# Retention attention with a bilinear feed-forward layer: slots 8 to 11 as one tile, two pairs of blocks by seven products in both four-slot tiles, and the order of all work written anew

## The chip, the cores and the metric

The kernel runs on one core of a Trainium2 chip. The metric is the device time of one execution in microseconds; the time of a kernel is the median of its runs. TensorE is called PE (its weight loads PEld), VectorE DVE, ScalarE ACT, GpSimd POOL, and SyncE, which issues the DMAs, SP.

## The reference

For each of 4 batches and 8 heads the attention runs a recurrence over 768 tokens with a head width of 64; its output is the input of the feed-forward layer.

```python
state = gamma[h] * state + k_t (outer) v_t          # 64 x 64, gamma[h] = 1 - 2**(-5-h)
y_t = (q_t @ state) / sqrt(64)                      # for each batch, head and token
x = y.transpose(0, 2, 1, 3).reshape(3072, 512)      # tokens x (heads * 64)
out = ((x @ w_a) * (x @ w_b)) @ w_out               # 512 -> 1536 -> 512, f32
```

## The kernel before

**Slots and tiles.** The 3072 tokens are 24 slots of 128, six to a batch. The feed-forward layer works on tiles of slots, TILES (line 16): 4, 2, 2, 2, 2, 4 and 8 slots, which are called tiles 0 to 6 here: tile 0 has slots 0 to 3, tile 1 slots 4 and 5, tile 2 slots 6 and 7, tile 3 slots 8 and 9, tile 4 slots 10 and 11, tile 5 slots 12 to 15, tile 6 slots 16 to 23.

**Attention of a slot.** k and q arrive by DMA as f32 and are multiplied by a table of powers of gamma into one bf16 tile `kqb` (`scaled`, lines 317 and 335); v is cast to bf16 (`vb`, line 287). SP's DMA transpose of `kqb` gives `kqT` (`flip`, line 376). On PE follow, for each slot:

- *scores*: 32 matmuls `at` (line 415) from `kqT`; DVE multiplies them by a mask into `aT` (line 421).
- *update*: 8 matmuls `st` (line 433) that add k times v to the state; a cast copies the state to `gst`.
- *inter*: 8 matmuls `y` from the state before (line 453); *intra*: 8 matmuls `y` from `aT` (line 463).
- *leave*: ACT copies `y` of a pair of slots into `xt`, the transposed input of the feed-forward layer.

`turn(new, old)` (line 477) writes these for a pair of new slots and a pair of old ones as one unbroken stretch of PE, a *burst*: update of `new`, scores of `new+1` and `new`, inter of both old slots, update of `new+1`, intra of both old slots, leave. The outputs of a pair are in the burst after the one that has its scores.

**Feed-forward.** d_ff is 12 blocks of 128. Of a block, `ffn_a` makes a with four matmuls over the tile's columns (line 619, 128 columns to a slot), which ACT copies to `asb` (line 622); `ffn_g` makes g (line 631), and DVE multiplies it by `asb` into `ht` (line 633). The banks of both come from a ring of three (line 78). The output is `ht` times w_out. For all tiles but the first this is done by seven products in place of eight (`Group`, line 717): `hs` are sums of quarters of `ht` (`hsum`, on POOL or DVE by an argument), `wsum` sums of quarters of w_out (`weight_sum`, on DVE), the products `mA`, `mB`, `mC` are matmuls of 256 columns (line 739), copied by ACT to `snaps` and added by DVE into `osb`, which `store` sends out.

**Seven products for x w_a and x w_b.** The same is done for two blocks at once (p and p+6) with halves of the tile. It needs sums of quarters of the weights (`weight_piece`, line 861, on POOL) and of the tile (`x_sum`, `xf_sum`, on DVE). Tile 6 does all six pairs of blocks so (`Unit`, `u`, line 913, 512 columns). Tile 5 does two of six pairs (`Quad`, line 1003, 256 columns), a and b apart; the remaining eight blocks are plain.

**Order.** The order on each engine is the order in which the program calls these functions, lines 1138 to 1297; `seq` ties each instruction to the one before it on its engine. The body is hand-written: `blocks(J, a, b)` writes a-blocks and g-blocks in turn, `casts(t)` the scaling of slot t, its transpose and the loads of slot t+2, `turn` a burst; `laced` writes tile 4's output between tile 5's Quads from the string LACED, and `big` the last part from the strings START and END. All scalings of slots 8 to 23 and most casts are on POOL.

```python
    turn(14, 12)
    hsum(4, 3, 0, 6, G_)
    weight_pieces(4)
    blocks(4, 6, 8)
    v_cast(16)
    blocks(4, 8, 9)
    hsums(4, 0, 3, G_)
    casts(18)
    blocks(4, 9, 10)
```

Of the kernel before, what the change touches and what calls it, by code (L numbers as in the profile page):

```python
# [9 lines left out]
F32 = mybir.dt.float32  # L10
# [5 lines left out]
TILES = [4, 2, 2, 2, 2, 4, 8]  # L16
# [3 lines left out]
START = ("A1 A2 u0.1 u1.1 A6 T X3 A7 B1 X2 A5 B6 B7 X1 A3 B5 u0.2 u1.2 B2 X4 A4 u0.6 B3 u1.6 B4 u0.5 u1.5 "  # L20
         "u0.7 u2.1 u0.3 u1.7 u2.6 u1.3 u0.4 u2.2 u3.1 u2.5 u1.4 u2.7 u3.6")
END = ("u11.1 u10.5 u10.7 u9.4 u11.6 u10.3 u11.2 S03 a1< u11.5 u11.7 u10.4 b1< u11.3 a1> b1> c1< d1< u11.4 a7 c1> d1> c2 d2 "
       "S02 S01 b7 a2 b2 S04 a6 b6 S13 a5 b5 S12 a3 b3 a4 b4 S11 c7 d7 c6 d6 S14 c5 d5 "
       "c3 c4 d4 d3")
V_LATE = range(12, 20)
LACED = ("X3 X2 m1 m7 m2 a1 b1 a2 b2 m6 X1 a6 b6 a7 b7 F2 X4 m5 a5 b5 K20 G2 a3 b3 a4 b4 V18 "
         "m3 c1 d1 F3 H3 c2 d2 c6 d6 c7 d7 c5 d5 m4 c3 d3 V19 c4 d4 G3")
# [4 lines left out]
def kernel(  # L32
# [78 lines left out]

    def raw_tile(shape, dtype, tag, name):
        return raw.tile(shape, dtype, tag=tag, name=name, bufs=3 if tag == "vf" else 2)
# [3 lines left out]
    def load_slot(t, names="kqv"):  # L117
        b, ci = divmod(t, NCH)
        for nm in names:
            src = {"k": k, "q": q, "v": v}[nm]  # L120
            if nm == "q":
                if t % 2 == 0:
                    load_two(nm, src, b, ci // 2, t)
                continue
            if t % 2 == 0:
                whole[nm] = raw_tile([P, 2, H, D], F32, nm + "f", nm + "f")
            raws[nm, t] = whole[nm][:, t % 2]
            s = src[b, :, ci * P : (ci + 1) * P, :].rearrange("h p d -> p h d")
            seq(nc.sync.dma_start(out=raws[nm, t], in_=s))

    def load_slots(t):
        for u, names in ((t, "kq"), (t + 1, "k"), (t, "v"), (t + 1, "v")):
            load_slot(u, names)
# [43 lines left out]
    def issue_loads(n):  # L177
        for _ in range(min(n, len(pending))):
            what = pending.pop(0)
            n = int(what[1:])  # L180
            if what[0] in "ab":
                load_wide(what[0], n)
            elif what[0] in "kqv":
                load_pair_q(n) if what[0] == "q" else load_two(what[0], {"k": k, "v": v}[what[0]], 0, n, 2 * n)
            else:
                {"p": load_pair, "s": load_slots, "t": load_slot, "w": load_w, "o": load_o}[what[0]](n)


    kqb = {}
# [113 lines left out]
    def cast_o(j):  # L303
        cast(nc.gpsimd, wo_bf[:, j * FPO : (j + 1) * FPO, :], wst["o", j])
# [12 lines left out]
    def scaled(eng, t, i):  # L317
        if i and t < 2 * PAIRS:
# [12 lines left out]
        else:  # L331
            dst = dst.rearrange("p hp r d -> p r hp d")
# [3 lines left out]

    def new_nat(t):
        kqb[t] = nat.tile([P, 2, HP, 2, D], BF16, tag="kqb", name="kqb")
        kb[t], qb[t] = kqb[t][:, 0], kqb[t][:, 1]
        vb[t] = nat.tile([P, H, D], BF16, tag="vb", name="vb")  # L340

    def casts(t, between=lambda: None):
        new_nat(t)
        scaled(nc.gpsimd, t, 0)
        between()
        scaled(nc.gpsimd, t, 1)
        if t not in range(12, 20):
            cast(nc.gpsimd, vb[t], raws["v", t])
        u = t + 2
        if u == 20:  # L350
            load_slot(u, "kq")
        flip(t)
        if u == 20:
            load_slot(u + 1, "k")
            return
        if u == 21:
            load_slot(u - 1, "v")
            load_slot(u, "v")
            load_slot(22, "kq")
            return  # L360
        if u in V_LATE:
            if u == 13:
                load_slot(12, "q")
            elif u == 19:
                load_slot(18, "kq")
            load_slot(u, {12: "k", 18: ""}.get(u, "kq"))
            if u % 2:
                load_slot(u - 1, "v")
                load_slot(u, "v")
        elif u < NSLOT:  # L370
            load_slot(u)

    def flip(t):
        if t % 2 == 0:
# [4 lines left out]

    def late_kq(t):  # L380
        for u in (t, t + 1):
            new_nat(u)
            scaled(nc.gpsimd, u, 0)
            scaled(nc.gpsimd, u, 1)
            flip(u)
        if t == 20:
            load_slot(23, "k")
            load_slot(22, "v")
            load_slot(23, "v")

    def casts_two(t):
        for u in (t, t + 1):
            new_nat(u)
            scaled(nc.gpsimd, u, 0)
            scaled(nc.gpsimd, u, 1)
            flip(u)
        for u in (t, t + 1):
            cast(nc.gpsimd, vb[u], raws["v", u])
        load_slot(t + 3)
# [9 lines left out]
    def scores(t, where, cuts=2):  # L409
        at = score_banks(where)  # L410
# [13 lines left out]
    def update(t, eng):  # L424
        ci = t % NCH
        if ci == NCH - 1:
            return
# [17 lines left out]

    def inter(t):
        if t % NCH == 0:
            return
        for j in range(2):
# [8 lines left out]
    def intra(t):  # L458
        for r in range(2):
# [7 lines left out]
    def leave(t):  # L467
        J, i = where[t]
# [7 lines left out]

    def turn(new, old, eng=nc.scalar):
        if old is not None:
# [844 lines left out]
```

## Time and profile before

| | before |
|---|---|
| time, median of 3 runs | 218.27 us (217.76 to 218.32) |
| the profiled execution's own time | 218.26 us |
| its span | 216.6 us |
| busy: PE, PEld | 209.8 us (97%), 145.8 us |
| busy: DVE, ACT, POOL | 151.1 us (70%), 105.1 us (49%), 155.5 us (72%) |
| granted TensorE clock | 1.00 |
| read from HBM, written | 28.31 MB, 6.29 MB |

The span runs from the first to the last instruction that the profile shows; the device time holds 1.66 us more. PE counts as busy from a matmul's start to its modelled end, and matmuls overlap, so a matmul's own length is longer than the distance from its start to the next one's start. The chain of waits follows the work that ended last backwards, at each step to what released it; its rows here are given in order of time with their length.

### The profile page before, as it was taken

What the parts mean: (1) busy time and instruction counts of PE and PEld (TensorE: products, weight loads), DVE (VectorE), ACT (ScalarE), POOL (GpSimd) and SP (SyncE); (2) the same over time, 40 slices, a digit from 0 to 9 for tenths busy, and PEclk for the clock granted to TensorE, in tenths of its full rate; (3) what the DMA queues carried; (4) which work ended last, traced back from release to release, by engine and by line L of the source; (5) the groups of instructions that cost most, each with busy time, mean ns of one, the idle gap of its engine ahead of it and who ended that gap; (6) DMA issues with size and microseconds to landing.
All of it is one profiled execution on the core that took longest, in us unless ns stands there. A gap on an engine that the chain in (4) does not pass through costs nothing.

```text
span 216.6 us, 5726 instructions
## 1 busy us (share of the span) xinstructions
PE 209.8 (97%) x2250; PEld 145.8 (67%) x2250; DVE 151.1 (70%) x277; ACT 105.1 (49%) x236; POOL 155.5 (72%) x187
## 2 busy tenths in 40 slices
PE   7789999999999999999999999999999999999994
PEld 3458445587458888888888877557864444458883
DVE  5796347845985486356377978686577887688952
ACT  3175325343224444464576475657545656652331
POOL 7277877778889487979959979799996999530000
PEclk9999999999999999999999999999999999999999
DMA  6999999999999999399989999980013000000055
GB/s 181 315 337 370 377 360 357 363 237 240 227 267 235 173 254 280 76 189 257 213 187 227 222 200 215 236 139 3 5 73 122 0 0 3 2 0 0 27 194 170
DMA packets 82906, 39.68 MB, mean 183 GB/s; under 512 B 57536, under 2 KB 75840, under 8 KB 82880
## 3 DMA queue, kind: packets, MB, share of 16 engines
q1 hardware_dynamic: 82736, 39.26, 74.4%
q8 instruction: 17, 0.28, 0.5%
q10 hardware_dynamic: 144, 0.07, 0.1%
q14 instruction: 9, 0.07, 0.1%
HBM read 28.31 MB, written 6.29 MB: 160 GB/s over the span
## 4 chain that ended last, share of the span: by engine, by line
PE 91%; SPq 3%; DMA 3%; POOL 0%; issue 0%; DVE 0%
PE a L619 18%; PE g L631 18%; PE mA L739 12%; PE uA L913 10%; PE mB L739 6%; PE o L656 5%; PE uB L913 5%; DMA wsta<-in_moe_w_a_dram 3%; PE mC L739 3%; PE at L415 2%; PE uC L913 2%; SPq L150 2%; PE y L463 2%; PE st L433 2%; PE fa L1003 2%; SPq L138 1%
## 5 line engine op out<-in xcount | busy, mean ns | idle before, releaser
L633 DVE TENSOR_TENSOR ht<-g,asb 128x256 bf16<-128x256 f32 (+1 forms) x70 | 34.4, 493 | 30.3 <-PE g L631 27.1
L619 PE MATMUL a<-xt,wa_bf 128*128 128x256 bf16 (+1 forms) x280 | 48.6, 300 | 0.2 <-POOL wa_bf L287 0.2
L631 PE MATMUL g<-xt,wb_bf 128*128 128x256 bf16 (+1 forms) x280 | 48.4, 300 | 0.0
L622 ACT CAST asb<-a 128x256 bf16<-128x256 f32 (+1 forms) x70 | 30.0, 428 | 33.5 <-PE a L619 31.3
L631 PEld LDWEIGHTS <-wb_bf 128*128 128x128 bf16 x280 | 27.1, 98 | 10.2
L619 PEld LDWEIGHTS <-wa_bf 128*128 128x128 bf16 x280 | 26.5, 98 | 10.8 <-POOL wa_bf L287 0.6
L920 ACT COPY snap<-uA 128x512 f32<-128x512 f32 x36 | 20.0, 587 | 15.4 <-PE uA L913 13.9
L335 POOL TENSOR_TENSOR kqb<-kf,ktab 128x512 bf16<-128x512 f32 x22 | 22.9, 1045 | 5.3 <-DMA kf<-in_k_dram 4.9
L739 PEld LDWEIGHTS <-hs 128*128 128x128 bf16 x234 | 22.8, 98 | 3.6
L421 DVE TENSOR_TENSOR aT<-at,mask 128x512 bf16<-128x512 f32 x36 | 22.3, 683 | 0.3
L335 POOL TENSOR_TENSOR kqb<-qf,qtab 128x512 bf16<-128x512 f32 x18 | 19.8, 1100 | 2.6 <-DMA qf<-in_q_dram 1.6
L672 POOL TENSOR_TENSOR ht<-gsb,asb 128x512 bf16<-128x512 bf16 x13 | 15.2, 1174 | 7.5 <-DVE gsb L672 7.4
L746 ACT COPY snaps<-mA 128x256 f32<-128x256 f32 x30 | 11.0, 374 | 18.9 <-PE mA L739 18.9
L672 POOL TENSOR_TENSOR hs<-ht 128x384 bf16<-128x384 bf16 (+3 forms) x14 | 15.8, 1130 | 5.7 <-DMA kf<-in_k_dram 3.2
L739 PEld LDWEIGHTS <-ht 128*128 128x128 bf16 x180 | 17.5, 98 | 3.3
L672 POOL TENSOR_TENSOR hs<-ht,hs 128x384 bf16<-128x384 bf16 (+1 forms) x17 | 16.8, 993 | 2.5 <-DVE ht L633 2.3
L739 PE MATMUL mA<-wsum,hs 128*128 128x256 bf16 x120 | 15.2, 273 | 0.0
L672 DVE TENSOR_TENSOR osb<-mB,snaps 128x256 f32<-128x256 f32 x20 | 8.4, 422 | 8.2 <-ACT snaps L746 4.3
L287 POOL CAST vb<-vf 128x512 bf16<-128x512 f32 x12 | 7.8, 668 | 5.2 <-DMA vf<-in_v_dram 5.2
L656 PE MATMUL o<-wo_bf,ht 128*128 128x512 bf16 x48 | 10.7, 379 | 0.0
L672 DVE TENSOR_TENSOR gsb<-uB,snap 128x512 bf16<-128x512 f32 x12 | 8.2, 686 | 2.9 <-ACT snap L920 2.1
L672 DVE TENSOR_TENSOR asb<-uB,snap 128x512 bf16<-128x512 f32 x12 | 8.2, 685 | 2.9 <-ACT snap L920 2.0
(148 smaller groups left out, 379.8 us busy)
## 6 DMA issues: line engine op xcount, KB each, us to landing
out_dram<-osb SPq DMA_DIRECT2D x21, 256.0 KB, 3.9
kf<-in_k_dram SPq DMA_DIRECT2D x18, 256.0 KB, 4.9
qf<-in_q_dram SPq DMA_DIRECT2D x9, 512.0 KB, 5.8
vf<-in_v_dram SPq DMA_DIRECT2D x18, 256.0 KB, 5.1
wsta<-in_moe_w_a_dram SPq DMA_DIRECT2D x6, 512.0 KB, 7.2
wsto<-in_moe_w_out_dram SPq DMA_DIRECT2D x6, 512.0 KB, 8.7
wstb<-in_moe_w_b_dram SPq DMA_DIRECT2D x5, 512.0 KB, 7.9
kf<-in_k_dram SPq DMA_DIRECT2D x3, 512.0 KB, 7.4
```

Of the source, the lines that this page charges most:

```text
L335: seq(eng.tensor_tensor(dst, src, tab, op=ALU.mult))
L421: seq(nc.vector.tensor_tensor(aT[t][:, r], at[r], mask.to_broadcast([P, HP, P]), op=ALU.mult))
L619: seq(nc.tensor.matmul(a, wa_bf[:, kt, fs], xcols(J, kt, c0, c1), start=(kt == 0), stop=(kt == KT - 1)))
L622: seq(nc.scalar.copy(asb, a))
L631: seq(nc.tensor.matmul(g, wb_bf[:, kt, fs], xcols(J, kt, c0, c1), start=(kt == 0), stop=(kt == KT - 1)))
L633: seq(nc.vector.tensor_tensor(ht[J][:, ft, c0:c1], g, asbs.pop((J, ft, c0)), op=ALU.mult))
L656: seq(nc.tensor.matmul(o, ht[J][:, ft, i * P : (i + 1) * P], wo_bf[:, ft], start=(ft == 0), stop=(ft == NFT - 1), skip_group_check=True))
L672: seq(eng.tensor_tensor(dst, x, y, op=op))
L739: seq(nc.tensor.matmul(m, w, right[:, j], start=(first and j == 0), stop=(j == NP - 1), skip_group_check=True))
L746: seq(nc.scalar.copy(self.snaps[:, n], self.bank["A"]))
L913: seq(nc.tensor.matmul(m, w, right[:, k], start=(first and k == 0), stop=(k == 1), skip_group_check=True))
L920: seq(nc.scalar.copy(self.snaps[n], self.bank["A"]))
```

## The change

**Tiles.** TILES is 4, 2, 2, 4, 4, 8: slots 8 to 11 are one tile (the new tile 3), whose blocks have 512 columns; slots 12 to 15 are tile 4 and slots 16 to 23 tile 5.

**Two of six pairs by products.** `Quad` is replaced by `Duo`, which is used in tiles 3 and 4 (pairs 0 and 1 of each). It has the a and the b product of a pair in one bank, 256 columns each, so that ACT copies, and DVE adds, 512 columns at once; a product of a and b is then one multiplication of the halves of `ab`, on DVE or POOL.

**Order.** One string, ORDER, gives all steps behind the start of tile 1, each step by a letter and numbers, and a loop calls a function for each. What `turn` wrote together are steps of their own: U update, S scores, I inter, N intra, L leave. So are k, y and v (scaling of k, of q, cast of v, with the engine: D for DVE, G for POOL, A for ACT), f (transpose), l (load), s (store), a and g (blocks), M (Group), d (Duo), u (Unit), h, x, X, W and w (the sums). `need` and `done` only assert at build time that a step stands behind those that it reads.

**Engines.** Eleven weight pieces and more `hs` sums than before are on DVE; one sum of w_out (W.1) is on POOL; four scalings (k of slot 6, q of slots 7, 10 and 17) are on ACT, where `scaled` writes eight multiplications of 128x64, and three (k of 17 and 22, q of 21) on DVE. The part before tile 1 is the same.

```diff
-TILES = [4, 2, 2, 2, 2, 4, 8]
+TILES = [4, 2, 2, 4, 4, 8]
...
+ORDER = """
...
+h.3.3.4.6.D s k.17.D l.k.19 s y.18.G g.3.11 g.3.10 h.3.4.0.4.D k.18.G f.17 M.3.0.7 l.q.20 h.3.2.4.6.G
+M.3.0.1 h.3.1.4.6.D h.3.4.4.6.D I.15 v.16.G I.14 N.14 f.18 l.v.19 l.q.22 U.15.A N.15 L.14 l.k.20 M.3.0.2
+l.v.20 M.3.0.6 y.19.G x.4.3.G k.19.G l.k.21 S.17.y.2 l.v.21 f.19 S.16.at.2 U.16.A M.3.0.5 l.k.22 x.4.2.D
...
     def scaled(eng, t, i):
...
+            if eng is nc.scalar:
+                for h in range(H):
+                    seq(nc.scalar.mul(dst[:, h % HP, h // HP, :], src[:, h, :], tab[:, h, :]))
+                return
...
-    def casts(t, between=lambda: None):
...
-    def turn(new, old, eng=nc.scalar):
...
-    def laced(order):
...
-    class Quad:
...
+    class Duo:
...
+        def product(self, bank, left, right, first):
+            if first:
+                pool, tag = self.tags[bank]
+                self.bank[bank] = pool.tile([P, 4 * P], F32, tag=tag, name="f" + bank)
+            p = self.p
+            for n, w_ in enumerate("ab"):
+                m = self.bank[bank][:, n * DH : (n + 1) * DH]
...
+                for k in range(2):
...
+                    seq(nc.tensor.matmul(m, w, right[:, k], start=(first and n == 0 and k == 0), stop=(k == 1),
+                                         skip_group_check=True))
...
+        def leave(self, i, c, bank, n):
+            ab = asbp.tile([P, 4 * P], BF16, tag="asb", name="ab")
+            tt(ab, self.bank[bank], self.snaps[n], ALU.add)
+            ft = NP * i + self.p
...
+            tt(ht[self.J][:, ft, c * DH : (c + 1) * DH], ab[:, :DH], ab[:, DH:], ALU.mult, self.engines["CBA".index(bank)
+               if bank == "C" else 1 + int(n == 1)])
...
-    def big():
...
-    turn(14, 12)
-    hsum(4, 3, 0, 6, G_)
-    weight_pieces(4)
-    blocks(4, 6, 8)
...
+    STEPS = {
+        "a": lambda J, ft: ffn_a(int(J), int(ft)),
...
+        "U": lambda t, e: update(int(t), engine[e]),
+        "S": lambda t, where, cuts: scores(int(t), where, int(cuts)),
+        "I": lambda t: inter(int(t)),
+        "N": lambda t: intra(int(t)),
+        "L": lambda t: leave(int(t)),
+    }
+    for step in ORDER.split():
+        kind, *args = step.split(".")
+        STEPS[kind](*args)
```

**Where instructions stand.** The rows give line, operation, output and inputs, and the shape; left-out rows are "...".

*PE, where the scores of slots 14 and 15 are.* Before, in `turn(14, 12)` behind a 256-column block of tile 4 (`g` with `wb_bf`): the update of 14 (`st`) opens the burst, the scores of 15 (`at_2174`) follow, and those of 14 and the outputs of 12 and 13 come behind them.

```order
L631 LDWEIGHTS wb_bf
L631 MATMUL g<-xt,wb_bf 128x256
L433 LDWEIGHTS kqb
L433 MATMUL st<-vb,kqb 64x64
...
L415 LDWEIGHTS kqT
L415 MATMUL at_2174<-kqT 64x128
L415 LDWEIGHTS kqT
L415 MATMUL at_2175<-kqT 64x128
```

Now, behind a 512-column block of tile 3: the scores of 15 (`at_2102`) and the update of 14 stand alone between two blocks; the scores of 14 and what was left of the outputs of 12 and 13 are in a burst three blocks ahead (S.14 I.13 N.12 N.13 U.13 in ORDER).

```order
L657 LDWEIGHTS wb_bf
L657 MATMUL g<-xt,wb_bf 128x512
L445 LDWEIGHTS kqT
L445 MATMUL at_2102<-kqT 64x128
...
L467 LDWEIGHTS kqb
L467 MATMUL st<-vb,kqb 64x64
...
L644 LDWEIGHTS wa_bf
L644 MATMUL a<-xt,wa_bf 128x512
```

One turn has become two bursts. Counted over the program behind 42 us, the bursts are 11 before and 16 now, and the places where one kind of matmul follows another in or beside a burst are 39 before and 47 now.

*SP, round the transpose of slot 17* (the second `DMA_TRANSPOSE` before, the first now). Before:

```order
L129 DMA kf<-in_k_dram 128x8x64
L138 DMA qf<-in_q_dram 128x8x128
L376 DMA_TRANSPOSE kqT<-kqb 128x8x128
L129 DMA kf<-in_k_dram 128x8x64
L376 DMA_TRANSPOSE kqT<-kqb 128x8x128
L129 DMA vf<-in_v_dram 128x8x64 x2
```

Now:

```order
L188 DMA vf<-in_v_dram 128x8x64
L188 DMA kf<-in_k_dram 128x8x64
L425 DMA_TRANSPOSE kqT<-kqb 128x8x128
L198 DMA qf<-in_q_dram 128x8x128
L425 DMA_TRANSPOSE kqT<-kqb 128x8x128
```

The load behind the transpose of slot 17 is now a q load of two slots, in place of v loads of one slot each.

*DVE, where k of slot 17 is scaled now* (`kqb` from `kf`). It was on POOL, between products of `ht` and the scalings of other slots.

```order
L659 TENSOR_TENSOR ht<-g,asb 128x512
L451 TENSOR_TENSOR aT<-at_2102,mask 128x512
L451 TENSOR_TENSOR aT<-at_2103,mask 128x512
L659 TENSOR_TENSOR ht<-g,asb 128x512
L696 TENSOR_TENSOR hs_1991<-ht 128x512
L403 TENSOR_TENSOR kqb<-kf,ktab_376 128x2x4x64
L659 TENSOR_TENSOR ht<-g,asb 128x512 x2
```

It stands behind the masks of slot 15, the product of block 5 and an `hs` sum.

606 lines of the change are left out of this document (249 added, 357 removed).

## The prediction

> **What bounds the kernel now.** I read the page first: the busy shares, the slices, and the split of the chain of work that ended last.
>
> ```profile
> span 216.6 us, 5726 instructions
> PE 209.8 (97%) x2250; PEld 145.8 (67%) x2250; DVE 151.1 (70%) x277; ACT 105.1 (49%) x236; POOL 155.5 (72%) x187
> PE   7789999999999999999999999999999999999994
> PE 91%; SPq 3%; DMA 3%; POOL 0%; issue 0%; DVE 0%
> ```
>
> PE is busy from the fourth slice to the last and makes 91% of the chain. PE never lets another engine onto the path, so the time is the sum of its stream: what each matmul takes, what a change between kinds of matmul costs, and the few short waits. The table by stage asks the same of the other engines (pairs: busy us, instructions; PE, PEld, DVE, ACT, POOL).
>
> ```profile
> 42.00:60.00 18.00, 18.00 (x132) 12.79 (x132) 12.51 (x21) 5.63 (x14) 14.36 (x16) 1.00 1.10 240
> 60.00:96.00 36.00, 35.99 (x448) 29.91 (x447) 22.18 (x45) 16.37 (x41) 27.85 (x33) 1.00 1.09 213
> 118.00:148.00 30.00, 30.00 (x386) 20.10 (x386) 24.50 (x46) 18.32 (x43) 27.29 (x30) 1.00 0.98 196
> 195.00:216.60 21.60, 18.42 (x171) 15.99 (x168) 14.82 (x27) 5.66 (x16) 0.00 (x0) 1.00 0.28 98
> ```
>
> PE fills every stage at a granted clock of 1.00. POOL is the next fullest (27.29 of 30.00), then DVE (24.50 of 30.00); ACT has room. A move from POOL to DVE or ACT therefore gains nothing by itself; it can only prevent or cause waits of PE. I work against the profiled execution, 218.26 us with 216.6 of span; the median of the runs is 218.27, so no correction is needed. All PE rows up to a(1,0), at about 42 us, and the last 85 are the same in both kernels, and so is what follows the last matmul; the change acts between.
>
> **Full-size matmuls.** The chain in order of time has long runs, from which one matmul is read: 7.77/36 = 0.2158 us at 512 columns, 3.93/36 = 0.1092 at 256.
>
> ```profile
> 52.75 7.77 PE o L656 x36
> 201.60 3.93 PE mA L739 x36
> ```
>
> Slots 8 to 11 as two tiles took 2 x 12 blocks x (a, g) x 4 = 192 matmuls of 256 columns. As one tile they take 8 plain blocks x 2 x 4 = 64 of 512, and two pairs of blocks by products: 2 x 2 weights x 7 x 2 = 56 of 256. The other four-slot tile had its two pairs already. So -192 x 0.1092 + 64 x 0.2158 + 56 x 0.1092 = -20.97 + 13.81 + 6.12 = **-1.04 us**.
>
> **Switches of shape.** The attention matmuls use part of the array: st and the last y are 128*64, at and the first y 64*64, all else 128*128. From the timeline of PE (start, its own length, line):
>
> ```profile
> 35.37 1.03 PE L619 MATMUL a<-xt,wa_bf 128*128 128x512 bf16 x4
> 36.33 0.64 PE L538 MATMUL at<-kqT 64*64 64x128 bf16 x32
> 36.90 0.82 PE L631 MATMUL g<-xt,wb_bf 128*128 128x512 bf16 x3
> ...
> 131.97 1.03 PE L631 MATMUL g<-xt,wb_bf 128*128 128x512 bf16 x4
> 132.93 0.32 PE L433 MATMUL st<-vb,kqb 128*64 128x64 bf16 x8
> 133.18 0.64 PE L415 MATMUL at<-kqT 64*64 64x128 bf16 x32
> 133.65 0.39 PE L453 MATMUL y<-kqT,gst 64*64 64x128 bf16 x16
> 133.97 0.32 PE L433 MATMUL st<-vb,kqb 128*64 128x64 bf16 x8
> 134.12 0.62 PE L463 MATMUL y<-aT,vb 128*64 128x128 bf16 x16
> 134.67 1.04 PE L619 MATMUL a<-xt,wa_bf 128*128 128x512 bf16 x4
> 135.54 1.03 PE L631 MATMUL g<-xt,wb_bf 128*128 128x512 bf16 x4
> ```
>
> Read from start to start. Four full matmuls take 0.87 (134.67 to 135.54), but 0.96 when a burst of attention follows (131.97 to 132.93; 35.37 to 36.33 too). Eight st take 0.15 when the shape stays (133.97) and 0.25 when it changes behind them (132.93). Thirty-two at take 0.47 with their own shape behind them (133.18) and 0.57 with a full matmul behind them (36.33). So a switch costs about 0.10 where it is plainly seen; the entry into 64*64 adds a few hundredths within the at. I take 0.12.
>
> The order counts them behind the first 42 us: before, 11 bursts with 39 switches; now, 16 bursts with 47, since a pair's update, scores and outputs no longer stand in one turn. The 8 more are 4 into 64*64 from full, 3 back, and 1 into st. 8 x 0.12 = **+0.96 us**. The bounds are nothing (if a switch costs only where something else is short) and 8 x 0.15 = 1.2. The matmuls in the bursts are the same in kind and number.
>
> The Trainium skill, TensorEngine Tiling (Array Packing), Key Properties, says that a change of the tiling mode, and not only of the tile, drains the TensorE; it gives no price. By that rule each added switch pays, and the sum has the +0.96; without it, nothing. The 0.10 at each kind of boundary above agrees with the rule.
>
> **Waits that go.** PE's own short waits show in the chain as runs longer than their like: 0.44 is four matmuls of 256, 0.57 a run of at between full matmuls.
>
> ```profile
> 43.03 0.55 PE a L619 x4
> 43.58 0.44 PE g L631 x4
> ...
> 80.62 0.66 PE at L415 x32
> 99.65 0.51 PE g L631 x4
> 113.02 0.51 PE g L631 x4
> 113.53 0.55 PE a L619 x4
> 116.27 0.66 PE at L415 x32
> ```
>
> 0.11 + 0.09 + 0.07 + 0.07 + 0.11 + 0.09 = 0.54 us. All lie in tiles of 256 columns, where a block must get its bank back in a few 0.44s. Three lie in tiles 3 and 4 of before, whose blocks become 512 wide. There the bank's work per block grows less than PE's:
>
> ```profile
> L633 DVE TENSOR_TENSOR ht<-g,asb 128x512 bf16<-128x512 f32 x18 | 12.3, 690 | 10.0 <-PE g L631 9.8
> L622 ACT CAST asb<-a 128x512 bf16<-128x512 f32 x18 | 10.6, 586 | 13.4 <-PE a L619 12.6 <-issue 0.6
> ```
>
> 0.690 and 0.586 stand against 4 x 0.2158 = 0.86. The others stand next to an attention burst whose neighbours are now different. I credit **-0.45**; the ends are -0.54 and 0, if as many come back elsewhere.
>
> **A wait that comes: the transpose of slot 17.** Before, k and q of slot 17 were scaled on POOL; now k is on DVE behind ht of block 5 and an hs sum, and the transpose follows in SP's queue. PE's steps between the end of g.3.5 and the scores of 17 are a.3.11, g.3.11, g.3.10 (12 x 0.2158 = 2.59), four products M.3.0 (24 x 0.1092 = 2.62), and a burst of 16 y from gst, 16 y and 8 st (0.32 + 0.55 + 0.15, and 0.10 to enter): 6.33 us. Against it:
>
> ```profile
> L672 DVE TENSOR_TENSOR hs<-ht 128x512 bf16<-128x512 bf16 x1 | 1.0, 1043 | 0.0
> L335 DVE TENSOR_TENSOR kqb<-kf,ktab 128x512 bf16<-128x512 f32 x2 | 1.3, 688 | 0.6 <-DMA kf<-in_k_dram 0.6
> DMA to landing us min/median/max: 3.0/4.5/6.0
> ```
>
> 0.69 + 1.04 + 0.69 = 2.42 and a landing of 3.0, 4.5 or 6.0 make 5.4, 6.9 or 8.4: a wait of 0, 0.6 or 2.1. DVE's operations overlap by some hundredths, so I take **+0.3**. Behind PE's wait stands all that follows, and nothing gives it back.
>
> **Edits that I cost at nothing.** Five weight pieces move from POOL to DVE between 42 and 60 us; at the 1.04 of the hs row they add 5.2 to DVE's 12.51 of 18, while one of four output-weight sums leaves it. That cover is gone if such a piece takes over 1.1 us more. Four scalings go to ACT in eight pieces of 64 columns. No row shows those; the nearest is this one at 128:
>
> ```profile
> L805 ACT COPY osb<-mA 128x128 f32<-128x128 f32 x1 | 0.3, 265 | 1.3 <-PE mA L800 1.3
> ```
>
> Between 8 x 0 and 8 x 0.265 = 2.1 us each I take 1.7; ACT was busy 16.37 of 36 between 60 and 96. Where a cast of a-block follows such a set, PE can lose some tenths; what hides it is the three banks of the ring. The loads issued earlier have buffers to fill only when the scalings have read them, as before. At the end the hs sums of slots 20 to 23 stand in another order on DVE, each done before its product in the same positions; no time.
>
> Sum: 218.26 - 1.04 + 0.96 - 0.45 + 0.3 = **218.0 us**.
>
> **Rivals.** *Switches nearly free.* If an added switch costs little, because the lone bursts fall where a drain hides, and slot 17 lands in 3 to 4 us, the sum is 218.26 - 1.04 - 0.45 = 216.8, and half the price gives 217.2. For: the added ones are of kinds of which before has few. Against: the 0.10 stands above at both entries into a burst and behind the st and the at of it.
>
> *Slot 17 late (slower).* The landing of 6.0, the largest of 18, makes the wait 2.1 instead of 0.3: 219.8. It decides for slower from a landing of about 5.2. For: a load of 512 KB of q is issued right behind it. Against: no load is issued in the microseconds ahead.
>
> *DVE behind.* In the pair of slots 16 and 17 four masks, two xf sums and the Duo's additions come close together. Two bf16 sums show what POOL at work does to DVE:
>
> ```profile
> L672 DVE TENSOR_TENSOR hs<-ht 128x768 bf16<-128x768 bf16 x2 | 2.3, 1132 | 0.0
> L672 DVE TENSOR_TENSOR hs<-ht 128x1536 bf16<-128x1536 bf16 x4 | 3.8, 952 | 0.1
> ```
>
> Half the columns took longer beside a working POOL than twice as many at the end, where POOL did nothing. If three such sums each come 0.5 late ahead of a product, 219.5. The Trainium skill, GPSIMD Engine Reference, Specifications, states that GpSimd's SBUF interface is shared with VectorE, with contention when a DVE instruction has two SBUF inputs; every moved sum has two. These rows agree.
>
> *It does not do what it says:* the waits of 0.54 return in the same number, 218.5.
>
> **How the numbers follow.** The forecast, 217.6 to 218.6 with its own bounds, has 0.48; switches nearly free 0.27; slot 17 late 0.13; DVE behind 0.08; the waits return 0.04. A measurement of this kernel tells about 0.3%, 0.65 us, from no change. Faster than that takes the first rival and a little of the forecast: 0.30. Slower takes the two late ones and a part of the forecast's upper end: 0.23. Between them 0.47. The range cuts off the far half of the first rival and the far end of the late ones: 217.1 to 219.3.
>
> **What would show it.** Right: PE still over 95% busy; start to start 0.96 ahead of each lone burst; the span at 216.3; no run of 0.51 or 0.55 in the new tile 3. The first rival: four full matmuls ahead of a burst at 0.87. The second: a gap of PE over 0.5 at the scores of slot 17, ended by DMA kqT. The third: gaps ended by DVE xf or ab. The forecast is wrong if PE stands still anywhere for over 0.7 us, or if a lone burst costs under half of what the rows say.

## The result, and the profile after

The changed kernel takes 218.91 us (median of 22 runs, 218.23 to 220.22) where the kernel before takes 218.07 (22 runs): ratio 1.0043, 95% interval 1.0029 to 1.0057. It is slower by 0.8 to 0.9 us. The time lies in the stated range, 217.1 to 219.3; but the sum of the prediction, 218.0, is level with before, and the kernel is slower by more than the interval. Its profiled execution was one of its longer ones, 219.68 us, so a second profile of the same kernel (218.59 us) is used beside it. The ratios leave out runs that count as disturbed, and the medians given with the experiments include them.

The page of the changed kernel: span, busy shares, and the split of the chain that ended last.

```profile
span 217.9 us, 5509 instructions
PE 208.7 (96%) x2162; PEld 138.1 (63%) x2178; DVE 162.1 (74%) x286; ACT 108.5 (50%) x246; POOL 139.1 (64%) x160
PE 72%; DMA 10%; POOL 6%; SPq 4%; issue 4%; DVE 1%; ACT 1%; POOLq 0%; DVEq 0%; ACTq 0%
```

PE is as busy as before, 96% for 97%, and this number hides the whole loss. The chain shows that there is one: PE was 91% of it and is 72%; DMA and POOL have 16%. It does not show its size: the second profile, 1.1 us shorter, has PE at 83%. By stage (columns as before: pairs of busy us and instructions for PE, PEld, DVE, ACT, POOL):

```profile
42.00:60.00 18.00, 17.87 (x161) 12.54 (x163) 12.54 (x22) 9.46 (x30) 14.33 (x13) 1.00 0.99 220
60.00:96.00 36.00, 35.54 (x436) 27.78 (x427) 27.11 (x47) 18.66 (x47) 27.44 (x27) 1.00 1.06 234
96.00:118.00 22.00, 21.41 (x290) 12.86 (x293) 18.89 (x33) 11.32 (x27) 14.98 (x15) 1.00 1.11 210
118.00:148.00 30.00, 29.22 (x324) 19.69 (x324) 23.95 (x42) 16.78 (x35) 17.72 (x21) 1.00 0.89 181
```

PE stands still for 0.46 us in the second row, 0.59 in the third and 0.78 in the fourth, where before it was busy for 35.99, 22.00 and 30.00. (The counts of matmuls are not to be compared, for some records are missing: the fourth row has 324 of PE, and e8 below, with the same order, 391.) POOL has far less work in the fourth (17.72 for 27.29), and yet POOL waits longer than before, as its waits from 42 to 148 us show, first before, then after (engine, line, what it waited for: total us, times, longest):

```profile
POOL kqb L335 <- DMA kf<-in_k_dram: 3.6, 4, 1.5
POOL kqb L335 <- DMA qf<-in_q_dram: 1.6, 3, 0.7
```

```profile
POOL kqb L403 <- DMA kf<-in_k_dram: 7.6, 4, 4.9
POOL kqb L403 <- DMA qf<-in_q_dram: 6.3, 3, 3.6
```

The scalings of k and q waited for their loads 5.2 us in all before, none over 1.5, and 13.9 now, up to 4.9. These rows are only those in which the profile names a load ahead of a scaling; before, it also names a load of k ahead of one `hs` sum and one product of `ht`, which read no k (3.2 and 1.4 us). POOL and DVE run in order, so what stands behind such a scaling is late with it. PE's three longest waits for another engine between 42 and 200 us, first profile:

```profile
PE g L657 <- DVE ht L696: 0.5, 1, 0.5
PE mA L758 <- POOL hs L696: 0.4, 1, 0.4
PE fB L1007 <- DVE xf L696: 0.2, 1, 0.2
```

Behind each of them a scaling stood for its load. Each row of the timelines below has its start, its length, and in brackets the idle time ahead of it and who ended it. **The hs sum** (the second of the three waits), in the second profile, POOL and then PE:

```profile
111.90 1.04 POOL L403 TENSOR_TENSOR kqb<-qf,qtab 128x512 bf16<-128x512 f32 x1 [3.52 <-DMA qf<-in_q_dram]
112.90 1.49 POOL L403 TENSOR_TENSOR kqb<-kf,ktab 128x512 bf16<-128x512 f32 x1
114.35 1.33 POOL L696 TENSOR_TENSOR hs<-ht,hs 128x512 bf16<-128x512 bf16 x1
```

```profile
114.43 0.60 PE L758 MATMUL mA<-wsum,hs 128*128 128x256 bf16 x4
115.74 0.39 PE L758 MATMUL mA<-wsum,hs 128*128 128x256 bf16 x2 [0.71 <-POOL hs L696]
```

y.18 waits 3.52 us for the load of q 18; k.18 and the sum h.3.2.4.6 stand behind it, and the fifth matmul of M.3.0.6 needs that sum. From start to start PE lost 0.87 us here (1.31 for 4 x 0.109), and 0.55 in the first profile. There the profile puts the same wait of y.18, 3.19 us, down to a matmul of PE; but the load of q 18 was issued at 105.69 and took 6.4 us to land, and y.18 began at 112.23, 0.14 behind the landing, as in the second profile.

Next on PE stand the scores of 17, and in the second profile their transpose was as late as the sum (PEld is PE's weight load):

```profile
116.16 0.48 PEld L445 LDWEIGHTS <-kqT 64*64 64x64 bf16 x32 [0.31 <-DMA kqT<-kqb]
```

The transpose was issued at 110.82 and landed 5.3 us later, at 116.12. PE lost another 0.10 for it (0.42 from the fifth matmul to the scores, 0.32 in the first profile), and it would have lost the whole 0.98 at the scores if the sum had been in time, for they could not begin before 116.16. So in this profile one of the two waits hides the other. In the first profile the transpose took 4.1 us and landed at 115.57, 0.27 ahead of where PE would have been without the wait for the sum. **k 22** on DVE, first profile:

```profile
132.17 1.23 DVE L403 TENSOR_TENSOR kqb<-kf,ktab 128x512 bf16<-128x512 f32 x1 [1.95 <-DMA kf<-in_k_dram]
...
133.66 0.41 DVE L696 TENSOR_TENSOR ht<-fA,asb 128x256 bf16<-128x256 f32 x1
134.12 0.81 PE L657 MATMUL g<-xt,wb_bf 128*128 128x512 bf16 x3 [0.51 <-DVE ht L696]
```

DVE stood 1.95 us for the load of k 22, a slot whose scores PE reaches at 148, and the product that gives PE its bank back (133.66) came after it. From start to start PE lost 0.68. **The xf sum**, first profile:

```profile
81.98 1.04 POOL L403 TENSOR_TENSOR kqb<-qf,qtab 128x512 bf16<-128x512 f32 x1 [2.07 <-DMA qf<-in_q_dram]
...
83.93 1.05 DVE L696 TENSOR_TENSOR hs<-ht,hs 128x384 bf16<-128x384 bf16 x1 [1.29 <-POOL hs L696]
...
86.19 1.02 DVE L696 TENSOR_TENSOR xf<-xf,xt 128x512 bf16<-128x512 bf16 x1
86.21 0.38 PE L1007 MATMUL fB<-xf,wea 128*128 128x256 bf16 x2 [0.25 <-DVE xf L696]
```

Two hand-overs: y.12 waits for q 12, the sum h.2.2 stands behind it on POOL, h.2.4 on DVE waits for h.2.2, and the xf sums stand behind h.2.4. PE lost 0.41.

The whole difference can be laid out in a sum. From the starts of all matmuls behind 42 us I took, for each kind, the number times the steady distance (0.2158, 0.1092, and 0.014 to 0.028 for those of attention), at each change of shape the usual extra of its kind (0.09 to 0.12), and called the rest waiting. The waits are thus what is left over; that the steady distances hold is seen apart from the sum, 0.216 and 0.109 in the median of all four profiles:

| us | before | after | after, second | e8 below |
|---|---|---|---|---|
| own time | 218.26 | 219.68 | 218.59 | 217.95 |
| tile 1 starts at | 41.99 | 41.76 | 41.49 | 42.00 |
| matmuls at steady distance | 165.97 | 164.93 | 164.93 | 164.93 |
| changes of shape | 39: 4.13 | 47: 4.90 | 47: 4.90 | 47: 4.90 |
| waits | 0.82 | 2.70 | 1.92 | 0.71 |

### The profile page after: what moved, and what is told of

Read it like the earlier page. It is cut to its first block, busy times and chain, and to the rows that moved or that the text cites. A ratio compares the mean times of both kernels' runs of the same rounds, so it can differ in the third digit from the quotient of the medians.

```text
span 217.9 us, 5509 instructions
## 1 busy us (share of the span) xinstructions
PE 208.7 (96%) x2162; PEld 138.1 (63%) x2178; DVE 162.1 (74%) x286; ACT 108.5 (50%) x246; POOL 139.1 (64%) x160
## 4 chain that ended last, share of the span: by engine, by line
PE 72%; DMA 10%; POOL 6%; SPq 4%; issue 4%; DVE 1%; ACT 1%; POOLq 0%; DVEq 0%; ACTq 0%
PE g L657 14%; PE a L644 13%; PE uA L908 9%; PE mA L758 9%; PE o L680 5%; PE uB L908 5%; DMA kf<-in_k_dram 4%; PE mB L758 4%; DMA wsta<-in_moe_w_a_dram 3%; POOL kqb L403 3%; DMA qf<-in_q_dram 3%; PE uC L908 2%; PE mC L758 2%; SPq L210 2%; POOL hs L696 2%
## 5 line engine op out<-in xcount | busy, mean ns | idle before, releaser
L659 DVE TENSOR_TENSOR ht<-g,asb 128x256 bf16<-128x256 f32 (+1 forms) x54 | 29.3, 550 | 17.5 <-PE g L657 16.1
L657 PE MATMUL g<-xt,wb_bf 128*128 128x256 bf16 (+1 forms) x213 | 40.3, 323 | 0.7 <-DVE ht L696 0.5
L644 PE MATMUL a<-xt,wa_bf 128*128 128x256 bf16 (+1 forms) x211 | 40.3, 323 | 0.6 <-POOL wa_bf L347 0.2
L647 ACT CAST asb<-a 128x256 bf16<-128x256 f32 (+1 forms) x54 | 25.6, 478 | 23.3 <-PE a L644 18.6
L657 PEld LDWEIGHTS <-wb_bf 128*128 128x128 bf16 x216 | 20.6, 98 | 13.4 <-issue 1.0
L644 PEld LDWEIGHTS <-wa_bf 128*128 128x128 bf16 x216 | 20.3, 98 | 11.8 <-POOL wa_bf L347 0.5
L696 POOL TENSOR_TENSOR hs<-ht,hs 128x512 bf16<-128x512 bf16 (+2 forms) x10 | 12.2, 1225 | 6.6 <-DVE ht L659 4.2
L696 POOL TENSOR_TENSOR hs<-ht 128x768 bf16<-128x768 bf16 (+4 forms) x11 | 14.3, 1303 | 3.0 <-DVE ht L659 3.0
L520 ACT CAST xt<-y 128x512 bf16<-128x512 f32 x18 | 9.7, 592 | 6.0 <-PE y L494 3.5
L696 DVE TENSOR_TENSOR hs<-ht,hs 128x1536 bf16<-128x1536 bf16 (+4 forms) x10 | 10.3, 1034 | 3.1 <-POOL hs L696 3.0
```

Of the source, the lines that this page charges most:

```text
L644: seq(nc.tensor.matmul(a, wa_bf[:, kt, fs], xcols(J, kt, c0, c1), start=(kt == 0), stop=(kt == KT - 1)))
L647: seq(nc.scalar.copy(asb, a))
L657: seq(nc.tensor.matmul(g, wb_bf[:, kt, fs], xcols(J, kt, c0, c1), start=(kt == 0), stop=(kt == KT - 1)))
L659: seq(nc.vector.tensor_tensor(ht[J][:, ft, c0:c1], g, asbs.pop((J, ft, c0)), op=ALU.mult))
L696: seq(eng.tensor_tensor(dst, x, y, op=op))
```

## The experiments

The theory after the result, A: matmuls and switches nearly cancel, as forecast, and the loss is PE's waits for steps that stand behind a wait for a load. The rival B: the stream of PE itself got longer, by dearer switches; later D: the engines have no room left anywhere; and, in e10 and e15, E and G: PE waits at the scores of 17 for their transpose.

**e1_waits: three steps moved.**

```diff
- N.11 h.2.4.0.3.D N.10 ... x.3.1.D d.3.0.7
+ N.11 N.10 ... x.3.1.D d.3.0.7 h.2.4.0.3.D
- h.3.4.0.4.D k.18.G ... h.3.2.4.6.G M.3.0.1 h.3.1.4.6.D
+ h.3.2.4.6.D k.18.G ... h.3.4.0.4.D M.3.0.1 h.3.1.4.6.G
- k.23.G k.22.D ... g.4.3 f.22
+ k.23.G ... g.4.3 k.22.D f.22
```

> The changed kernel with three steps moved on DVE and POOL, nothing moved on PE: the sum h.2.4 (pieces 0 to 3) behind the xf sums of the new tile 3; the sum h.3.2.4.6 given to DVE and h.3.1.4.6 to POOL; the scaling k.22 (DVE) from before block g.4.2 to behind g.4.3. Theory A (the loss is three waits of PE, each behind a step that itself waits for a load): the waits of 0.41, 0.55 and 0.68 us in the profiled execution go, about 0.7 to 1.2 us in the median, so 217.7 to 218.2, level with the kernel before. Theory B (the matmul stream of PE itself became longer, by its 8 added switches of shape, and the waits are an accident of one execution): 218.7 to 218.9 as the changed kernel.

Measured: 220.19, ratio 1.0083 (1.0063 to 1.0103). Slower than the changed kernel by another 0.9 us by the ratios, 1.3 by the medians: both theories missed. Its waits of PE:

```profile
PE a L644 <- DVE ab L696: 0.6, 1, 0.6
PE st L467 <- DVE gst L347: 0.6, 1, 0.6
PE st L467 <- POOL vb L347: 0.3, 1, 0.3
```

The three old waits are gone or halved, and three others stand a few steps on, each behind a step that I had moved: `ab` behind h.2.4, the copy of the state behind k 22, the cast v 16 behind h.3.1. The wait of an engine that runs in order has to leave the place, not change it.

**e2_split: nine switches added to the kernel before.** The update of 12, 14 and 20 a block earlier, the intra matmuls of 12, 16 and 18 a block later.

```diff
-    blocks(4, 5, 6)
-    turn(14, 12)
+    turn(14, 12, part="f")        # update(14)
+    blocks(4, 5, 6)
+    turn(14, 12, part="m")        # scores, inter, update(15)
...
+    blocks(4, 6, 7)
+    turn(14, 12, part="t")        # intra, leave
```

> The kernel before with four bursts cut apart and no other change: the first update of a burst one block earlier (bursts of 12, 14 and 20) and the intra matmuls one block later (bursts of 14, 18 and 20). 9 more switches of shape (48 for 39), the same matmuls. Theory A (a switch costs 0.10 to 0.11 us on PE): 9 x 0.105 = +0.95, 219.0. Theory B (an added switch drains more and costs 0.2 or over): +1.8 or more, 219.9 and up. If a switch were nearly free: 218.1.

Measured: 219.38, ratio 1.0065 (1.0053 to 1.0078), +1.37 us. In its profile a lone update between two blocks:

```profile
108.68 0.60 PE L631 MATMUL g<-xt,wb_bf 128*128 128x256 bf16 x4
109.21 0.32 PE L433 MATMUL st<-vb,kqb 128*64 128x64 bf16 x8
109.45 0.61 PE L619 MATMUL a<-xt,wa_bf 128*128 128x256 bf16 x4
```

0.53 from g to st for 4 x 0.109, so 0.09; 0.24 from st to a for 0.15, so 0.09. Counted over the whole profile the nine cost 1.0 us, 0.11 each; the two profiled executions differ by 1.10, and the medians by 0.15 a switch. What the rest of the medians' difference is was not seen. B, with 0.2 and over, is out as the profile counts it, and so is a switch that costs nothing. By the drain on a change of tiling mode (the Trainium skill, TensorEngine Tiling (Array Packing), Key Properties) each must pay; these rows agree.

**e3_plain3: tile 3 without products.**

```diff
- d.3.0.1 x.3.2.D x.3.1.D d.3.0.7 M.2.0.6 d.3.0.2
+ a.3.0 g.3.0 M.2.0.6 a.3.6
```

> The changed kernel with the two pairs of blocks of the new tile 3 as plain blocks (no Duo and no xf sums there). PE gets 32 matmuls of 512 columns for 56 of 256: 32 x 0.2158 - 56 x 0.1092 = +0.79 us. Theory A: +0.79, less the wait of about 0.4 at the first xf product that goes with them: 219.2 to 219.7. Theory C (the products of tile 3 give back in waits what they save): 218.9 or less.

Measured: 221.01, ratio 1.0132 (1.0117 to 1.0147). The matmuls are +0.79 as worked out and PE's stream ends 0.75 after that of the first profile; the hs sum of M.3.0.6 cost 1.2, and the last stores left 1.1 us later behind PE's end; the cause of that stays open. C is out by the time and by PE's stream, which has the 0.79. What the products of tile 3 are worth in the time is not measured by it, as the kernel lost over twice as much and part of that has another cause.

**e4_merge: four switches taken out of the changed kernel.**

```diff
- U.12.D d.3.1.3 a.3.8 S.13.y.2
+ d.3.1.3 a.3.8 U.12.D S.13.y.2
- S.14.at.2 I.13 N.12 N.13 U.13.D ... S.15.y.2 U.14.A
+ U.13.A S.15.ff.2 S.14.at.2 I.13 U.14.A N.12 N.13
```

> The changed kernel with three lone steps put back beside others: the update of 6 to the scores of 6 and 7, the update of 12 to the scores of 13, the scores of 15 and the update of 14 into the burst with the scores of 14. 43 switches of shape for 47. Theory A (0.105 each): -0.42, 218.5. Theory B (an added switch costs 0.2 or over): -0.8 or more, 218.1 and down. If a switch were nearly free: 218.9.

Measured: 220.77, ratio 1.0112 (1.0072 to 1.0152). Four switches fewer show in the count, but the hs sum made PE wait 1.0 us, the transpose of 17 another 0.6 right behind it, and then the clock went down (windows; the last column but two is the granted clock):

```profile
118.00:119.00 1.00, 1.00 (x44) 0.83 (x33) 0.77 (x2) 0.31 (x1) 1.00 (x2) 0.99 1.40 84
119.00:120.00 1.00, 1.00 (x7) 0.67 (x6) 1.00 (x2) 0.32 (x2) 1.00 (x2) 0.50 1.17 260
121.00:122.00 1.00, 1.00 (x6) 0.73 (x5) 0.38 (x2) 0.37 (x1) 0.00 (x0) 0.50 1.09 285
```

No verdict on the switches; it shows what a longer wait costs behind itself.

**e5_loads, e6_loads_merge, e7_loads_start: loads ahead of transposes.** e5 moves the loads; e6 has the merges of e4 as well, e7 tile 1's blocks in turn.

```diff
- f.9 ... l.k.12 f.10 k.12.G f.11 l.q.12 l.k.13
+ l.k.12 f.9 l.q.12 l.k.13 ... f.10 k.12.G f.11
- a.3.9 f.16 ... l.k.18 ... l.q.18
+ a.3.9 l.k.18 l.q.18 f.16
- f.17 ... f.18 l.v.19 l.q.22 ... l.k.20 ... l.k.21
+ f.17 l.k.20 l.k.21 ... f.18 l.v.19 ... l.q.22
```

> The changed kernel with loads moved ahead in SP's queue, to where their buffers are already free: k and q of slot 12 to either side of the transpose of 9, k and q of 18 ahead of the transpose of 16, k of 20 and 21 right behind the transpose of 17, k of 22 ahead of the transpose of 19; and the scaling of q of 22 two places later on POOL. PE's order and the engines of all work stay. Theory A2 (the loads stand in SP's queue behind transposes, which wait for scalings, which wait for loads; POOL falls behind, and its sums make PE wait): POOL no longer waits over 2 us for k 12, q 18 and q 22, the PE waits of 0.41, 0.55 and 0.68 go, and none takes their place: 217.6 to 218.2, with the spread of the kernel before. Theory D (POOL and DVE have too much to do between the bursts; the waits move on whatever the loads do, as they did when three steps were moved): 218.8 or more.

> The same with the three merges of bursts as well (43 switches of shape for 47). Theory A2 and 0.105 a switch: 0.4 under the kernel with the loads alone, 217.2 to 217.8. If the bigger burst of slots 14 and 15 makes a wait of its own: level with the loads alone or over it.

> The same loads, and the blocks of tile 1 in turn (a, g, a, g) instead of five a blocks ahead. The waits at 41.8 to 48.7 us (0.12 + 0.24 + 0.10 in the changed kernel, 0.11 before) should fall to the 0.1 of before: 0.3 under the kernel with the loads alone. If the weight pieces on DVE are their cause and not the order of the blocks: level with it.

Measured: 222.82, 220.94 and 221.89; ratios 1.0199, 1.0131 and 1.0180, the lowest bound 1.0110. All far slower. POOL no longer waited for k 12, but PE waited for transposes, in e5 and then in e6:

```profile
PE at L445 <- DMA kqT<-kqb: 3.1, 2, 2.0
```

```profile
PE at L445 <- DMA kqT<-kqb: 2.4, 2, 1.3
```

They are the scores of slot 11 and of slot 17. The transposes themselves (duration of the issue on SP, ns min/median/max; us to landing; then the issue of those of 10 and 11) in the changed kernel and in e5:

```profile
L425 SPq DMA_TRANSPOSE kqT<-kqb x18: 1231/1732/3576, 52.7 to 139.9; - x18
...
DMA to landing us min/median/max: 3.1/4.1/5.6
```

```profile
73.34 3.31 SPq L425 DMA_TRANSPOSE kqT<-kqb  x2
```

```profile
L425 SPq DMA_TRANSPOSE kqT<-kqb x18: 1232/1830/4350, 53.0 to 142.9; - x18
...
DMA to landing us min/median/max: 3.2/4.9/6.5
```

```profile
74.11 5.70 SPq L425 DMA_TRANSPOSE kqT<-kqb  x2
```

With loads ahead of them the two transposes of 10 and 11 took 5.70 us of issue for 3.31; over all 18 the median issue went from 1.73 to 1.83 us, and landing from 4.1 to 4.9. So loads and transposes trade margins on one queue, and A2, that the loads only had to come earlier, is wrong. In e7 the blocks in turn met another wait, behind the eight small scalings on ACT:

```profile
PE g L657 <- ACT asb L647: 0.9, 1, 0.9
```

Five a blocks ahead cost 0.34 more than before at 42 to 49 us, but in that order the scalings on ACT cost nothing.

**e8_behind: the order on SP left, the waits left where they are, and what stood behind them taken ahead.**

```diff
- y.12.G U.9.A N.8 N.9 I.8 h.2.2.0.3.G ... h.2.1.0.3.G
+ U.9.A N.8 N.9 I.8 h.2.2.0.3.G ... h.2.1.0.3.G y.12.G
- y.18.G g.3.11 g.3.10 h.3.4.0.4.D ... h.3.2.4.6.G M.3.0.1 h.3.1.4.6.D ... v.16.G
+ v.16.G y.18.G g.3.11 g.3.10 h.3.2.4.6.D ... h.3.4.0.4.D M.3.0.1 h.3.1.4.6.G
- y.22.G M.3.0.4 v.17.G y.20.G
+ M.3.0.4 v.17.G y.20.G y.22.G
- k.23.G k.22.D ... f.22 N.17 U.18.D ... S.18.at.2
+ k.23.G ... N.17 U.18.D ... S.18.at.2 k.22.D f.22
```

> The changed kernel with the steps that PE or DVE wait for taken from behind POOL's and DVE's waits for loads, loads and transposes left in their places in SP's queue (but for the transpose of 22, which goes with its scaling): q of 12 scaled behind the two hs sums of tile 2 that stood behind it; the cast v 16 ahead of the scaling of q 18, the sum h.3.2.4.6 on DVE and h.3.1.4.6 on POOL in its place; q of 22 scaled behind v 17 and q 20; k of 22 scaled behind the masks of 18 and 19. Theory A (the loss is PE's waits for steps behind a wait for a load): PE waits under 1.1 us in all from 42 us on, against 2.7 in the changed kernel's profile and 0.8 before; 217.7 to 218.3, and a spread of about 0.6 as before. Theory D (the engines beside PE have no room left; the waits come back elsewhere): 218.8 or more.

> The kernel with the steps taken from behind waits for loads once more, unchanged, for a second profile: its first one was of 217.95 us and had no wait of PE, while its runs lie between 217.95 and 219.51. Theory A (its PE stream is the forecast's, and what is above 218.0 is waits of PE on DMA): the span less the switches and the matmuls is again in waits, at one to three places, and the place tells which transfer is late; 218.0 to 219.5. Theory F (a matmul or a switch takes longer in some executions): no place with over 0.2, the excess spread over all.

> The kernel with the steps taken from behind waits for loads a third time, unchanged, for the profile of one of its longer executions (two profiles had no wait and 217.95 and 218.12). Theory G: a longer one waits at the scores of 17 for their transpose. Theory D: it waits in many places.

Three profiles: 217.95, 218.12 and 217.62 us. The first one's chain and its third stage:

```profile
PE 91%; SPq 3%; DMA 3%; issue 0%; POOL 0%; ACT 0%; DVE 0%
```

```profile
118.00:148.00 30.00, 30.00 (x391) 20.10 (x388) 23.46 (x44) 16.44 (x35) 18.23 (x21) 1.00 0.88 181
```

PE is 91% of the chain again and has no gap in the stage; all three have no wait over 0.26 behind 42 us, and the first is within 0.1 of 218.26 - 1.04 + 0.77. So for these executions A holds: 47 switches, the new tile and the products together are no slower than before. POOL itself still waited 11.4 us for loads in the first of them (13.9 in the changed kernel): what counts is what stands behind the wait. Beside this execution, in which PE has the same order, the changed kernel's first profile loses 1.98 us from tile 1 to the end, 1.64 of it at the three waits. The timed runs do not show the loss gone: median 219.00 of 12 (217.95 to 219.51), as in the changed kernel, and ratio 1.0020 (0.9991 to 1.0049), an interval that holds both 1 and the changed kernel's 1.0043. The three profiled executions are as short as the shortest of these runs, so what the longer ones wait for was not seen. The margin at the scores of 17 is small even in them: the transpose landed 0.33, 0.09 and 0.72 us ahead.

**e14_after_again: the changed kernel's second profile.**

> The changed kernel once more, unchanged, for a second profile: its first was of 219.68 us, over its median of 218.91. Theory A: the same three places (xf sum at 86 us, hs sum from POOL at 115, k 22 at 133) with other lengths, 0.6 to 1.6 us in all. Theory F: as above.

218.59 us. Of the three waits the hs sum is there with 0.87 and the scores of 17 behind it with 0.10, the xf sum with 0.08, k 22 not at all. The waits differ from execution to execution with the landing of loads and transposes; F, longer matmuls everywhere, is out.

**e15_hs_dve: the hs sum alone** (the second pair of lines of e8's diff).

> The changed kernel with one of the moves alone: the sum h.3.2.4.6, for which PE waited 0.55 us in the first profile and 0.98 in the second, on DVE, h.3.1.4.6 on POOL for it, and the cast v 16 ahead of the scaling of q 18. Theory A3 (this sum, behind the scalings of 18 that wait for the load of q 18, is the steady wait of the changed kernel, the others come in some executions only): 0.5 to 1.0 under the changed kernel, 217.9 to 218.4. Theory G (the wait only passes to the scores of 17 behind it, whose transpose is as late): 218.7 to 219.

Measured: 218.82, ratio 1.0036 (1.0016 to 1.0057), not to be told from the changed kernel's 1.0043. Its profile (218.83) has no wait at M.3.0.6 and none at the scores of 17, whose transpose landed 0.18 ahead, so G does not hold in this execution; but two waits stand at a bank that DVE gives back late, the first behind k 22 at 133 us, where PE lost 0.50, the second in tile 1 at 49.7 us:

```profile
PE g L657 <- DVE ht L696: 0.3, 1, 0.3
PE g L657 <- DVE ht L659: 0.3, 1, 0.3
```

A3 is wrong in its size: taking this wait away alone does not move the median. G forecast 218.7 to 219, and by the second profile of the changed kernel an execution like that one would have gained nothing; whether the other executions are of that kind was not seen.

**e9_behind_merge and e17_two_merges: e8 with four and with two switches fewer.**

> The same with the three merges of bursts (43 switches of shape for 47). Theory A and 0.105 a switch: 0.4 under the one without the merges, 217.3 to 217.9, under the kernel before. If the bigger burst of slots 14 and 15 brings a wait: level or slower.

> The kernel with all steps taken from behind waits for loads, and two of the merges: the update of 6 to the scores of 6 and 7 and that of 12 to the scores of 13 (45 switches for 47). Theory A: 2 x 0.105 less than without, 217.75 where that one's profiles had 217.95 and 218.12, median 217.8 to 218.8 with the same spread. If an update that comes later delays the state: a wait of PE at the outputs of 7 or 13.

e9: ratio 1.0018 (0.9981 to 1.0056), median 220.38, runs from 217.84 to 225.24. e17: 1.0029 (1.0005 to 1.0052), median 219.00, profiled 217.75, the 0.2 under e8's first profile that two switches should give (and 0.13 over its third). Inconclusive on the switches in the median: a fifth of a microsecond drowns in runs that differ by two. In the profiled execution of e9, 222.24 us, PE stood 2.45 us at the scores of 17 for their transpose, which took 2.96 us of issue and landed 6.8 us after it began.

**e10_flip17, e11_flip17_merge, e12_flip_only, e18_k17_early: slot 17.** k of 17 on POOL where it stood idle; in the first three the transpose of 17 earlier on SP as well; e11 with merges, e12 on the changed kernel, the others on e8.

```diff
- h.3.1.0.4.G h.3.2.0.4.G ... l.q.18 ... k.17.D ... k.18.G f.17
+ k.17.G h.3.1.0.4.G h.3.2.0.4.G ... l.q.18 f.17 ... k.18.G
```

> The last kernel without the merges (steps taken from behind waits for loads, 47 switches), and with k of slot 17 scaled on POOL ahead of the sums h.3.1 and h.3.2, where POOL stands idle for 3 us, and the transpose of 17 right behind the load of q 18, some 4 us earlier in SP's queue. Its profile without the move had no wait of PE and gave 217.95, but its other runs went up to 219.5. Theory E (what differs from run to run is the landing of the transpose of 17, which PE's scores of 17 meet at about 116 us, as where they waited 2.5 us in the kernel with the merges): 217.8 to 218.2 in nearly all runs, median 218.0. Theory D (any of many steps can be late; one more margin is not enough): 218.7 or more, with a spread over 1 us.

> The same, and the update of 6 and of 12 merged as before, and the burst of slots 14 and 15 as one, at the later of its two places (43 switches). Theory A with 0.105 a switch: 0.4 under the one without the merges, 217.5, which beats the kernel before. Theory D: over 218.5.

> The changed kernel with the transpose of 17 and the scaling of its k moved in that way, and nothing else. Theory E: the waits behind loads stay (0.4 at the xf sum, 0.4 to 1.0 at the hs sum on POOL, 0.7 at k 22) and only the 17th transpose's part goes: 218.4 to 218.8. If that transpose were the whole of it: 218.0. If it is not late in the changed kernel, where the wait for the hs sum stands ahead of it: 218.9.

> The kernel with the steps taken from behind waits for loads, and k of slot 17 scaled on POOL in its idle 3 us ahead of the sums h.3.1 and h.3.2; the order in SP's queue is left alone, so the transpose of 17 can be issued as soon as the queue comes to it, about 1.3 us earlier than at 111.2. Theory E (the longer executions wait at the scores of 17): median 217.9 to 218.4 where it was 219.0, highest under 219. Theory D (many margins of some tenths, so that one more does not settle it): 218.7 to 219.2 with the same spread.

Measured: 223.92, 224.90, 219.13 and 223.17; ratios 1.0243, 1.0265, 1.0032 (1.0019 to 1.0045) and 1.0208. e12 neither helps nor harms. The other three met a wait that has nothing to do with slot 17's transpose, on ACT in e10:

```profile
133.19 0.59 ACT L1020 COPY snapf<-fA 128x512 f32<-128x512 f32 x1 [5.38 <-DMA out_dram<-osb]
```

The last snap of the second Duo takes an `osb` buffer. In e10 it is one whose store is issued only behind the transpose of 19 in SP's queue, and PE waits 3.6 us for the snap; in e8 the snap had no such wait. That it gets another buffer because k 17 is on another engine is an inference; no profile shows it. Theory E is thus not tested by these three. e12 and e15 take away one each of the two waits that stand together at 116 us, the transpose and the sum, and neither gains; that is what one would see if each hides the other, but e8 leaves the transpose alone too, and no run takes both away without a new wait.

## Why the prediction was wrong, step by step

- **Full-size matmuls, -1.04:** right. The table's 165.97 to 164.93 is the same product of numbers and steady distances; that the distances held is seen in the profiles, and e3 gives 0.79 back for its part.
- **Switches of shape, +0.96:** the mechanism right, the size a little high by the profiles. +0.77 for the eight in the table, 0.10 each, where I took 0.12; e2 has 0.11 in its profile and 0.15 in its medians.
- **Waits that go, -0.45:** these did go as placed: no run of 0.51 or 0.55 is left in the new tile 3. But tile 1, whose waits I let go with the others, has 0.45 at 42 to 49 us where it had 0.11, for its five a blocks ahead.
- **A wait that comes, +0.3 at the scores of 17: this is the step that failed.** As put, one wait comes, for a transpose, worked out from the busy times of DVE and a landing, and it is the only one that the sum adds. Its working holds: from the end of g.3.5 the transpose was issued 2.09 us later (2.42 in the sum), PE has 6.45 us of steps (6.33), and the landing of 4.1 and 5.3 us makes no wait in the first profile and 0.9 in the second, where PE paid 0.10 of it openly and the rest under the wait for the hs sum. But three others came that I had not priced: 0.55 and 0.87 at M.3.0.6, 0.68 and nothing behind k 22, 0.41 and 0.08 at the xf sum. In all, PE waited 1.88 and 1.10 us more than before, where the sum had 0.15 less. The place of the first is the one that I had looked at, a microsecond ahead of the scores of 17; I had summed DVE's work there and not asked what POOL waits for.
- **Edits costed at nothing:** "the loads issued earlier have buffers to fill only when the scalings have read them, as before" looks at the loads from the wrong side. The scalings wait for the loads, 13.9 us for 5.2, and POOL's smaller sum of work says nothing on that. The scalings in eight pieces on ACT took 2.0 us each where I took 1.7, and no wait of PE in the changed kernel is put down to them.
- **Rivals:** the nearest by place was DVE behind, with 0.5 late ahead of a product, on the xf sum among others. Its mechanism was contention, which no run here isolates; the runs show a wait for a load handed on from engine to engine. Slot 17 late is in the second profile, hidden; with moved loads or merged bursts (e4, e5, e6, e9) it stands in the open.
- **What would show it:** PE still over 95% busy and a lone burst at 0.96 both came true, and neither could have told of the loss. Of the signs of being wrong, PE standing still for over 0.7 us came only in the second profile, and there by a hair (0.71). The chain's split and the waits of POOL told of it.

Together: -1.04 + 0.77 + 1.88 (2.70 for 0.82) - 0.23 for the earlier start = +1.38 for the measured +1.42 of the two profiled executions. In the second profile 1.10 of more waiting and an earlier start by 0.50 leave +0.33. Both sums close because the waits are what is left over. Shown is that the first profile lost its time at three waits behind loads, and that profiled executions without them are level with before. Not shown is that these waits make the 0.84 of the medians: e8 takes them away in its profiles, and its median did not come down. Which waits make up the longer executions, of the changed kernel and of e8, stays open; the transpose of 17 is a candidate by its margins, and untested. No version was found that is faster than before beyond its interval.

## What to carry to other kernels

When a step moves to another engine or place, ask not only when it is needed but what it waits for and what stands behind it there: on an engine that works in order, a scaling early for its own purpose, waiting for a load, delays every sum behind it. Read the helpers' waits for DMA, and what stands behind each, and the chain's split by engine; the busy shares of PE and POOL both looked as good as before. Where two waits meet at one place, the longer hides the other, and taking one away may show nothing. And a queue that carries loads, transposes and stores has one margin to share: each move of loads here was paid for by a transpose.

## What the runs showed of the hardware

A wait of PE costs more than itself when it is long. In e5, behind a wait of 1.95 us for a transpose:

```profile
79.00:82.00 3.00, 1.05 (x45) 0.80 (x44) 0.93 (x3) 0.37 (x1) 2.50 (x4) 1.00 0.99 243
82.00:83.00 1.00, 1.00 (x48) 0.79 (x38) 0.73 (x2) 0.61 (x2) 0.84 (x1) 0.62 0.97 205
83.00:84.00 1.00, 1.00 (x9) 0.73 (x6) 1.00 (x2) 0.74 (x2) 0.00 (x0) 0.50 1.18 275
84.00:85.00 1.00, 1.00 (x7) 0.69 (x6) 0.75 (x2) 0.42 (x2) 0.00 (x0) 0.50 0.94 254
```

The granted clock is 0.50 for 3.4 us (82.25 to 85.66 in the trace's record of the clock), and eight matmuls of 256 columns that take 0.87 took 1.68. In e4 waits of 1.0 and 0.6 close together did the same, for 3.4 us again; in e6 one of 1.26 did not. The Trainium skill, TensorE: Matmul & The Clock Gate, What's actually happening, has the clock halve after an idle window of about 3.4 us; here less than 2 us were enough, and the measurement decides.
